# Contiguous rows between the gate and the output projection, and half of the x1*x3 products on GpSimd

## The chip, the cores and the metric

The kernel runs on one core of a Trainium2 chip. The core has five engines that run at the same time, each with a queue that it works off in order: PE (TensorE, the matrix engine; PEld is its weight load, which overlaps with matmuls), DVE (VectorE), ACT (ScalarE), POOL (GpSimd) and SP (which issues the DMAs here). PE writes to PSUM, which has 8 banks of 512 fp32 elements in each of 128 partitions; DVE and ACT read PSUM, and GpSimd works on SBUF alone here. The metric is the device time of one launch in microseconds.

## The reference, cut to what matters

Two layers follow each other, for 4 batches of 6272 positions and 256 channels.

```
f = lb + (1 - lb) * sigmoid(f_logit)
h = f[:, t] * h + (1 - f[:, t]) * x[:, t]        # for t = 0 .. 6271; all h kept
x1, x2, x3 = split(h_all @ w_proj, 3)            # 256 channels each
x2_conv = irfft(rfft(x2) * rfft(filter_fft))     # along the 6272 positions
out = (x1 * x2_conv * x3) @ w_out
```

## The kernel before

Each batch b goes through these steps.

`hgrn(b)` makes the recurrence in 13 chunks of 512 positions (the last has 128). For each chunk, f_logit and x are loaded (L275), ACT makes the sigmoid (L278), GpSimd the product with x (L280), PE turns both so that channels lie on partitions (L287), ACT makes f (L299) and DVE runs the scan over time (L304), once for each half of the channels. From the states, PE then makes x1 and x3 (L315). For each half of the channels, `jb`, ACT copies x1 out of PSUM into `x1s` with a scale (L323), which has two buffers, one for each `jb`; DVE multiplies x3, straight from PSUM, with it and writes `z` in fp16 (L326). `z` holds x1*x3 by channel and time, and has one buffer for each parity of b.

`phase_p(b)` projects to x2 with the time axis split as 128 x 49 (time = 49 m + r). `phase_f1`, `mini` and `units` make the convolution as products with small Fourier matrices, in 16 units of 8 channel pairs; the unit's product with the filter's spectrum is L658 on DVE, and its result goes into `Th` (L673, a copy at L246).

`phase_o(b)` does the rest, in 13 groups of up to four values of r: 12 full groups (rn = 4) and one of a single row (rn = 1). In a group, PE makes the last inverse transform for each row i of the group, with 4 matmuls of 64 partitions by 128 columns a row (L693). Before the change, row i's 128 results go to every rn-th PSUM column, beginning at column i: the order in PSUM is (m i), rows innermost. DVE multiplies with `z`, in which the rows of a group lie side by side too (time = 49 m + r), and writes `ys` (fp32 for PE's use), in the order (m i) as well (L700). PE projects with `w_out` (L710): for row i and each half of the channels, y[:, kh, :, i] is the 128x128 weight of one matmul with 256 columns, so the weight is read at steps of rn elements. ACT or DVE then copies the result out with a scale (L248, L253), and SP stores it (L719). `ys` has two buffers and so has the output.

The order of the work is written out by a planner, `Plan`, before the program is built. Every step is given with its cost on the engines that may do it, its readers and writers, and for PE steps the number of PSUM banks it takes. The planner runs a list schedule with these costs: at each step it takes the operation that can begin first (and among those the one with the longest way to the end), and emits it into its engine's queue. A PE step is emitted only if all that its readers need besides it is already emitted. Work of batch b+1 is thus mixed with units(b) and phase_o(b) where the order allows. The costs are written by hand: phase_o's product is counted at 0.08 + 0.27 us for each row of the group (1.16 us for four), its transform at 0.235 us a row, its projection at 0.34 us a row.

Of the kernel before, what the change touches and what calls it, by code (L numbers as in the profile page):

```python
# [9 lines left out]
F32 = mybir.dt.float32  # L10
# [3 lines left out]
AOP = mybir.AluOpType  # L14
# [12 lines left out]
CH = 512  # L27
# [19 lines left out]
def m0_of(r):  # L47
    return (128 * q_of(r) - r) // Q
# [135 lines left out]
def kernel(  # L184
# [10 lines left out]
    nc = tc.nc  # L195
# [4 lines left out]
    op = plan.op  # L200

    konst = ctx.enter_context(tc.tile_pool(name="konst", bufs=1))
# [22 lines left out]
    FL = konst.tile([128, NX, 4, D], F32, name="FL")  # L225
    fTs = konst.tile([128, 2, CH], F32, name="fTs")
    x1s = konst.tile([128, 2, CH], F32, name="x1s")
    dram = ctx.enter_context(tc.tile_pool(name="dram", bufs=1, space=bass.MemoryType.DRAM))

    H = [dram.tile([TB, 2, 2, UE * 64], F16, name=f"H{u}") for u in range(NU)]  # L230
    psp = ctx.enter_context(tc.tile_pool(name="psp", bufs=1, space=PSUM))
    PS = psp.tile([128, 8, 512], F32, name="PS")
# [25 lines left out]
    def either(n, runs=1.0):  # L258

        return {"ACT": 0.06 + runs * n / 1200.0, "DVE": 0.08 + runs * n / 960.0}  # L260
# [4 lines left out]
    def hgrn(b):  # L265
        z = zt[b % 2]
        for c in range(NCHK):
            t0 = c * CH
            nb = min(CH, S - t0) // 128
            n = nb * 128  # L270
            k = count["x"] % NX
            count["x"] += 1
            xt, ft = XT[:, k, 0:nb], FL[:, k, 0:nb]
            for dst, src, t in ((ft, f_logit, ("ft", k)), (xt, x, ("xt", k))):
                op({"SP": 0.5}, lambda e, dst=dst, src=src, t0=t0, n=n: nc.sync.dma_start(  # L275
                    dst, src[b, t0:t0 + n, :].rearrange("(j p) d -> p j d", p=128)),
                   w=[t], kb=n)
            op({"ACT": 0.1 + 0.213 * nb}, lambda e, ft=ft: nc.scalar.activation(  # L278
                ft, ft, AF.Sigmoid, scale=-1.0), w=[("ft", k)], table="sigmoid")
            op({"POOL": 0.1 + 0.535 * nb}, lambda e, xt=xt, ft=ft: nc.gpsimd.tensor_tensor(  # L280
                xt, xt, ft, op=AOP.mult), r=[("ft", k)], w=[("xt", k)])
            for kh in range(2):
                cols = slice(kh * 128, kh * 128 + 128)

                def turn(e, p, src, cols=cols, nb=nb):
                    for j in range(nb):
                        nc.tensor.transpose(PS[:, p, j * 128:(j + 1) * 128], src[:, j, cols],  # L287
                                            iden[:])
                sT = op({"PE": 0.108 * nb}, lambda e, p, f=turn, s=ft: f(e, p, s),
                        r=[("ft", k), "iden"], w=["qT"], take=1)  # L290
                uT = op({"PE": 0.108 * nb}, lambda e, p, f=turn, s=xt: f(e, p, s),
                        r=[("xt", k), "iden"], w=["qT"], take=1)
                j = count["f"] % 2
                count["f"] += 1
                fT = fTs[:, j, 0:n]
                t1 = HB[kh] + t0
                h = HA[:, t1:t1 + n]
                op({"ACT": 0.13 + n / 1200.0}, lambda e, p, fT=fT, n=n, kh=kh:
                   nc.scalar.activation(fT, PS[:, p, 0:n], AF.Identity,  # L299
                                        scale=nomc[:, kh:kh + 1], bias=1.0),  # L300
                   r=["om"], w=[("fT", j)], src=sT)
                init = 0.0 if c == 0 else HA[:, t1 - 1:t1]
                op({"DVE": 0.07 + 2.25 * n / 1000.0}, lambda e, p, h=h, fT=fT, n=n, init=init:
                   nc.vector.tensor_tensor_scan(h, fT, PS[:, p, 0:n], init, op0=AOP.mult,  # L304
                                                op1=AOP.add),
                   r=[("fT", j)] + ([("hn", kh, c - 1)] if c else []), w=[("hn", kh, c)],
                   src=uT)
            for jb in range(2):
                x13 = []
                for i in range(2):  # L310
                    js = slice(i * 256 + jb * 128, i * 256 + jb * 128 + 128)

                    def mm(e, p, i=i, js=js, t0=t0, n=n):
                        for kh in range(2):
                            nc.tensor.matmul(PS[:, p, 0:n], W13[:, kh, js],  # L315
                                             HA[:, HB[kh] + t0:HB[kh] + t0 + n],
                                             start=(kh == 0), stop=(kh == 1))
                    x13.append(op({"PE": 2 * n / 2400.0}, mm,
                                  r=[("hn", 0, c), ("hn", 1, c), "W13"], w=["qX"], take=1))
                j = count["s"] % 2  # L320
                count["s"] += 1
                xs, zz = x1s[:, j, 0:n], z[:, jb, t0:t0 + n]
                op({"ACT": 0.06 + n / 1200.0}, lambda e, p, xs=xs, n=n: nc.scalar.activation(  # L323
                    xs, PS[:, p, 0:n], AF.Copy, scale=ZS), w=[("x1s", j)], src=x13[0])
                op({"DVE": 0.07 + n / 960.0}, lambda e, p, zz=zz, xs=xs, n=n:
                   nc.vector.tensor_tensor(zz, PS[:, p, 0:n], xs, op=AOP.mult),  # L326
                   r=[("x1s", j)], w=[("z", b % 2, jb, c)], src=x13[1])

    def wraps():
        for kh, cuts in enumerate(((0, 1024, 2560, 4096, E0), (128, 2048, 3584, 5120, S))):  # L330
# [348 lines left out]
    def phase_o(b):  # L679
        zr = zt[b % 2][:].rearrange("p k (m r) -> p k m r", r=Q)  # L680
        tf = Th[:].rearrange("p c a g -> p (c a g)")
        for g, r0 in enumerate(range(0, Q, 4)):
            rn = min(4, Q - r0)

            def inv(e, cb, r0=r0, rn=rn):
                for i in range(rn):
                    r = r0 + i
                    sh = (128 - m0_of(r)) % 128
                    for rr in range(2):
                        c0 = (rr * Q + r) * 128  # L690
                        for p in range(2):
                            ps = slice(64 * p, 64 * p + 64)
                            nc.tensor.matmul(PS[:, cb + p, i:i + rn * 127 + 1:rn],  # L693
                                             tf[ps, c0:c0 + 128], ID[ps, rr, sh:sh + 128],
                                             start=(rr == 0), stop=(rr == 1))
            i1 = op({"PE": 0.235 * rn}, inv, r=[("Th", u) for u in range(NU)] + ["Th"], take=2)
            yk = g % 2
            y = ys[:, yk, :, 0:rn * 128].rearrange("p a (m i) -> p a m i", i=rn)
            op({"DVE": 0.08 + rn * 0.27}, lambda e, cb, y=y, r0=r0, rn=rn:
               nc.vector.tensor_tensor(  # L700
                   y, PS[:, cb:cb + 2, 0:rn * 128].rearrange("p a (m i) -> p a m i", i=rn),
                   zr[:, :, :, r0:r0 + rn], op=AOP.mult),
               r=[("z", b % 2, jb, c) for jb in range(2) for c in range(NCHK)],
               w=[("y", yk)], src=i1)

            def proj(e, ob, y=y, rn=rn):
                po = PS[:, ob:ob + 2].rearrange("m a (r e) -> m (a r) e", e=256)
                for i in range(rn):
                    for kh in range(2):
                        nc.tensor.matmul(po[:, i, :], y[:, kh, :, i], Wo[:, kh, :],  # L710
                                         start=(kh == 0), stop=(kh == 1))
            po = op({"PE": 0.34 * rn}, proj, r=[("y", yk)], take=2)
            k = count["o"] % 2
            count["o"] += 1
            op(either(256 * rn), lambda e, ob, k=k, rn=rn: copy(
                e, osb[k][:, 0:rn, :],
                PS[:, ob:ob + 2].rearrange("m a (r e) -> m (a r) e", e=256)[:, 0:rn, :], OS),
               r=[("x2o", i) for i in range(14)] if k else [], w=[("osb", k)], src=po)
            op({"SP": 0.5}, lambda e, k=k, r0=r0, rn=rn: nc.sync.dma_start(  # L719
                out[b].rearrange("(a r) d -> a r d", r=Q)[:, r0:r0 + rn, :],  # L720
                osb[k][:, 0:rn, :]),
               r=[("osb", k)] + ([("x2o", i) for i in range(14)] if k else []), kb=128 * rn)
# [8 lines left out]
    with tc.manual_schedule():  # L731
        with tc.tile_pool(name="tmp", bufs=1) as tmp:
            prepare(tmp)
            hgrn(0)
            wraps()
            plan.emit()
# [8 lines left out]
        ys = cv.tile([128, 2, 2, 512], F32R, name="ys")  # L745
# [47 lines left out]
```

## Time and profile before

| | us |
|---|---|
| median of 3 runs (lowest 652.3, highest 658.98) | 654.3 |
| the profiled execution | 655.55 |
| span of that execution's trace | 653.4 |
| PE busy in the span | 559.9 (86%) |
| DVE busy | 512.2 (78%) |
| ACT busy | 381.2 (58%) |
| POOL busy | 149.8 (23%) |

The span is what the trace covers; the execution's own time is 2.15 us longer. Busy times are sums over the whole span. An engine's work is the same in kind in each batch but lies in stages with different company: up to about 146 us the filter's transform and the first batch's recurrence and forward transform, then the units of a batch, its phase_o together with the next batch's recurrence, the forward transform, the next units, and so on, and from about 611 us the last phase_o by itself.

### The profile page before, as it was taken

The numbers are of one execution on the slowest core, as the hardware profiler recorded it, in microseconds if no ns is written. First come the engines' busy times: TensorE is split into PE (matmuls) and PEld (weight loads), VectorE is DVE, ScalarE is ACT, GpSimd is POOL, SyncE is SP. The second block draws the span as 40 slices with busy tenths as digits, with TensorE's granted clock in tenths as the row PEclk, the third lists the DMA queues.
The fourth block names the chain that finished last, engine by engine and source line by source line (L and its number), as shares of the span: only waits on it lengthen the run. The fifth ranks groups of instructions, "written<-read, shape, count | busy, mean of one in ns | idle before, by whom it ended". The sixth has DMA issues, their size and how long they took to land.

```text
span 653.4 us, 12392 instructions
## 1 busy us (share of the span) xinstructions
PE 559.9 (86%) x4821; PEld 430.0 (66%) x4821; DVE 512.2 (78%) x576; ACT 381.2 (58%) x490; POOL 149.8 (23%) x161
## 2 busy tenths in 40 slices
PE   3677888977799999897769999988789999968997
PEld 3455555764478886774538986954568887644786
DVE  7768787589978769699889467899987668999632
ACT  3788786794343558793445456964456567833333
POOL 5424420122104223213222132031023220011000
PEclk9989999899979999998898999999899999997898
DMA  8957755556659786435698588134598862055144
GB/s 310 382 178 256 237 164 172 178 170 192 179 167 333 245 300 211 146 129 180 196 266 266 180 276 282 65 97 148 159 258 293 301 219 108 1 162 160 41 186 170
DMA packets 77643, 130.09 MB, mean 199 GB/s; under 512 B 4878, under 2 KB 56146, under 8 KB 77586
## 3 DMA queue, kind: packets, MB, share of 16 engines
q1 hardware_dynamic: 77586, 129.31, 59.9%
q8 instruction: 38, 0.62, 0.4%
q14 instruction: 19, 0.16, 0.1%
HBM read 84.54 MB, written 32.11 MB: 179 GB/s over the span
## 4 chain that ended last, share of the span: by engine, by line
PE 53%; DVE 14%; DMA 13%; ACT 7%; issue 5%; POOL 2%; SPq 1%; DVEq 0%; ACTq 0%; POOLq 0%
PE PS L710 13%; PE PS L287 10%; PE PS L315 8%; DVE PP L658 8%; PE PS L693 6%; DMA FL<-in_f_logit_dram 6%; PE PS L589 5%; PE PS L668 3%; PE PS L604 2%; PE PS L648 2%; DVE HA L304 2%; ACT X L246 2%; DMA XT<-in_x_dram 2%; DMA H<-HA 2%; DMA Hu<-H 2%
## 5 line engine op out<-in xcount | busy, mean ns | idle before, releaser
L280 POOL TENSOR_TENSOR XT<-XT,FL 128x1024 f32<-128x1024 f32 (+1 forms) x52 | 116.4, 2238 | 266.4 <-DMA XT<-in_x_dram 117.6
L658 DVE TENSOR_TENSOR PP<-PS,Hu 98x1008 f16<-98x1008 f32 x128 | 145.6, 1200 | 8.9 <-PE PS L648 3.0
L246 ACT CAST X<-PS 128x784 f16<-128x784 f32 (+2 forms) x92 | 91.7, 1007 | 84.4 <-PE PS L668 77.2
L304 DVE TENSOR_TENSOR_SCAN HA<-fTs,HA,PS 128x512 f16<-128x512 f32 (+1 forms) x96 | 114.6, 1205 | 29.2 <-PE PS L287 20.7
L315 PE MATMUL PS<-HA,W 128*128 128x512 f16 (+1 forms) x416 | 106.5, 376 | 6.0 <-DVE HA L304 3.9
L299 ACT ACTIVATE fTs<-PS,nomc 128x512 f32<-128x512 f32 (+1 forms) x104 | 69.5, 669 | 65.2 <-PE PS L287 46.1
L710 PE MATMUL PS<-Wo,ys 128*128 128x256 f32 x392 | 102.5, 405 | 0.5 <-DVE ys L700 0.5
L710 PEld LDWEIGHTS PS<-Wo,ys 128*128 128x128 f32 x392 | 94.1, 325 | 5.6 <-issue 3.7
L700 DVE TENSOR_TENSOR ys<-PS,z 128x1024 fp32r<-128x1024 f32 (+1 forms) x52 | 60.6, 1178 | 42.0 <-PE PS L693 37.6
L668 PEld LDWEIGHTS <-PP 98*128 98x128 f16 x1024 | 55.8, 105 | 51.4 <-POOL PP L651 20.9
L668 PE MATMUL PS<-VA,PP 98*128 98x98 f16 x512 | 62.7, 220 | 21.7 <-DVE PP L658 9.9
L323 ACT ACTIVATE x1s<-PS 128x512 f32<-128x512 f32 (+1 forms) x104 | 59.0, 576 | 33.1 <-PE PS L315 23.7
L326 DVE TENSOR_TENSOR z<-PS,x1s 128x512 f16<-128x512 f32 (+1 forms) x104 | 66.4, 651 | 14.9 <-ACT x1s L323 10.4
L287 PE MATMUL PS<-iden,FL 128*128 128x128 f32 x392 | 67.1, 296 | 12.4 <-ACT FL L278 12.4
L287 PE MATMUL PS<-iden,XT 128*128 128x128 f32 x392 | 65.3, 289 | 8.9 <-POOL XT L280 7.3
L278 ACT ACTIVATE FL<-FL 128x1024 f32<-128x1024 f32 (+1 forms) x52 | 52.5, 1010 | 22.2 <-DMA FL<-in_f_logit_dram 22.1
L287 PEld LDWEIGHTS PS<-iden,XT 128*128 128x128 f32 x392 | 48.1, 148 | 25.2 <-POOL XT L280 10.4
L315 PEld LDWEIGHTS <-W 128*128 128x128 f16 x416 | 37.4, 100 | 39.3 <-issue 15.3
L668 PE MATMUL PS<-VB,PP 98*128 98x98 f16 x512 | 62.5, 220 | 0.0
L287 PEld LDWEIGHTS PS<-iden,FL 128*128 128x128 f32 x392 | 49.3, 152 | 19.6 <-ACT FL L278 9.8
L648 PE MATMUL PS<-HA,FT 64*128 64x512 f16 x256 | 41.8, 402 | 20.8 <-ACT X L246 19.2
L693 PE MATMUL PS<-ID,X 64*128 64x128 f16 x784 | 51.3, 309 | 1.0 <-ACT X L248 0.5
(90 smaller groups left out, 583.4 us busy)
## 6 DMA issues: line engine op xcount, KB each, us to landing
Hu<-H SPq DMA_DIRECT2D x64, 392.0 KB
FL<-in_f_logit_dram SPq DMA_DIRECT2D x48, 512.0 KB
XT<-in_x_dram SPq DMA_DIRECT2D x48, 512.0 KB
out_dram<-X SPq DMA_DIRECT2D x24, 512.0 KB
out_dram<-osb SPq DMA_DIRECT2D x24, 512.0 KB
HA<-in_moe_filter_fft_dram SPq DMA_DIRECT2D x12, 512.0 KB
HA<-HA SPq DMA_DIRECT2D x16, 384.0 KB
H<-HA SPq DMA_DIRECT2D x16, 196.0 KB
```

The lines of the kernel that those rows point to most:

```text
L246: nc.scalar.copy(dst, src)
L280: op({"POOL": 0.1 + 0.535 * nb}, lambda e, xt=xt, ft=ft: nc.gpsimd.tensor_tensor(xt, xt, ft, op=AOP.mult), r=[("ft", k)], w=[("xt", k)])
L287: nc.tensor.transpose(PS[:, p, j * 128:(j + 1) * 128], src[:, j, cols], iden[:])
L299: nc.scalar.activation(fT, PS[:, p, 0:n], AF.Identity, scale=nomc[:, kh:kh + 1], bias=1.0),
L304: nc.vector.tensor_tensor_scan(h, fT, PS[:, p, 0:n], init, op0=AOP.mult, op1=AOP.add),
L315: nc.tensor.matmul(PS[:, p, 0:n], W13[:, kh, js], HA[:, HB[kh] + t0:HB[kh] + t0 + n], start=(kh == 0), stop=(kh == 1))
L326: nc.vector.tensor_tensor(zz, PS[:, p, 0:n], xs, op=AOP.mult),
L658: nc.vector.tensor_tensor(PP[:TB, k, o, :, :, 1:64], px.unsqueeze(1).broadcast_to([TB, 2, UE, 63]), hh[:, :, :, 1:64], op=AOP.mult)
L668: nc.tensor.matmul(PS[:, ib + o, pr * TB:(pr + 1) * TB], PP[:TB, k, o, n, 2 * pr:2 * pr + 2, :], v[:TB], start=(n == 0), stop=(n == 1))
L693: nc.tensor.matmul(PS[:, cb + p, i:i + rn * 127 + 1:rn], tf[ps, c0:c0 + 128], ID[ps, rr, sh:sh + 128], start=(rr == 0), stop=(rr == 1))
L700: nc.vector.tensor_tensor(y, PS[:, cb:cb + 2, 0:rn * 128].rearrange("p a (m i) -> p a m i", i=rn), zr[:, :, :, r0:r0 + rn], op=AOP.mult),
L710: nc.tensor.matmul(po[:, i, :], y[:, kh, :, i], Wo[:, kh, :], start=(kh == 0), stop=(kh == 1))
```

## The change

Two things are changed. In `phase_o`, the rows of a group no longer lie interleaved: row i's results go to 128 adjoining PSUM columns, and `ys` has the order (i m), so that the weight of one projection matmul is contiguous. The product on DVE runs over the same elements in the same order, m outside and i inside, through views of the new layout. In `hgrn`, the product x1*x3 of the first half of the channels (jb = 0) is no longer made by DVE from PSUM: ACT copies x3 out of PSUM into a new tile `x3s` (one buffer), and GpSimd multiplies `x3s` with `x1s` and writes `z`. The second half stays on DVE. The planner is given costs for the two new steps, and its other costs are not changed.

```diff
@@ -225,6 +225,7 @@
     x1s = konst.tile([128, 2, CH], F32, name="x1s")
+    x3s = konst.tile([128, CH], F32, name="x3s")
@@ -322,9 +323,17 @@
                 xs, zz = x1s[:, j, 0:n], z[:, jb, t0:t0 + n]
                 op({"ACT": 0.06 + n / 1200.0}, lambda e, p, xs=xs, n=n: nc.scalar.activation(
                     xs, PS[:, p, 0:n], AF.Copy, scale=ZS), w=[("x1s", j)], src=x13[0])
-                op({"DVE": 0.07 + n / 960.0}, lambda e, p, zz=zz, xs=xs, n=n:
-                   nc.vector.tensor_tensor(zz, PS[:, p, 0:n], xs, op=AOP.mult),
-                   r=[("x1s", j)], w=[("z", b % 2, jb, c)], src=x13[1])
+                if jb:
+                    op({"DVE": 0.07 + n / 960.0}, lambda e, p, zz=zz, xs=xs, n=n:
+                       nc.vector.tensor_tensor(zz, PS[:, p, 0:n], xs, op=AOP.mult),
+                       r=[("x1s", j)], w=[("z", b % 2, jb, c)], src=x13[1])
+                else:
+                    x3 = x3s[:, 0:n]
+                    op({"ACT": 0.06 + n / 1200.0}, lambda e, p, x3=x3, n=n:
+                       nc.scalar.copy(x3, PS[:, p, 0:n]), w=["x3s"], src=x13[1])
+                    op({"POOL": 0.1 + 2.15 * n / 1000}, lambda e, zz=zz, xs=xs, x3=x3:
+                       nc.gpsimd.tensor_tensor(zz, x3, xs, op=AOP.mult),
+                       r=[("x1s", j), "x3s"], w=[("z", b % 2, jb, c)])
@@ -690,15 +699,15 @@
-                            nc.tensor.matmul(PS[:, cb + p, i:i + rn * 127 + 1:rn],
+                            nc.tensor.matmul(PS[:, cb + p, i * 128:(i + 1) * 128],
                                              tf[ps, c0:c0 + 128], ID[ps, rr, sh:sh + 128],
                                              start=(rr == 0), stop=(rr == 1))
             i1 = op({"PE": 0.235 * rn}, inv, r=[("Th", u) for u in range(NU)] + ["Th"], take=2)
             yk = g % 2
-            y = ys[:, yk, :, 0:rn * 128].rearrange("p a (m i) -> p a m i", i=rn)
+            y = ys[:, yk, :, 0:rn * 128].rearrange("p a (i m) -> p a m i", i=rn)
             op({"DVE": 0.08 + rn * 0.27}, lambda e, cb, y=y, r0=r0, rn=rn:
                nc.vector.tensor_tensor(
-                   y, PS[:, cb:cb + 2, 0:rn * 128].rearrange("p a (m i) -> p a m i", i=rn),
+                   y, PS[:, cb:cb + 2, 0:rn * 128].rearrange("p a (i m) -> p a m i", i=rn),
                    zr[:, :, :, r0:r0 + rn], op=AOP.mult),
```

## Rows read from the trace of the kernel before

**Rows 1.** Page, part 1: busy us, share of the span, instructions of each engine.

```profile
PE 559.9 (86%) x4821; PEld 430.0 (66%) x4821; DVE 512.2 (78%) x576; ACT 381.2 (58%) x490; POOL 149.8 (23%) x161
```

**Rows 2.** Busy time by stage: stretch and length, engines, clock granted, DMA share, GB/s.

```profile
core 0: us, PE busy (x) PEld busy (x) DVE busy (x) ACT busy (x) POOL busy (x), PEclk, DMA share, GB/s
185.00:262.00 77.00, 76.13 (x562) 61.61 (x560) 60.44 (x62) 43.75 (x64) 22.34 (x12) 0.98 0.76 256
...
345.00:407.70 62.70, 61.70 (x467) 51.28 (x465) 42.20 (x44) 34.11 (x48) 16.73 (x8) 0.97 0.75 254
437.00:471.70 34.70, 26.63 (x295) 16.06 (x296) 34.70 (x38) 14.81 (x22) 4.74 (x15) 0.96 0.47 151
471.70:547.20 75.50, 73.27 (x585) 59.75 (x584) 55.84 (x59) 44.70 (x63) 20.33 (x12) 1.00 0.77 256
```

**Rows 3.** Timeline of the last phase_o: start and length in us, count, idle before.

```profile
634.69 1.94 PEld L710 LDWEIGHTS PS<-Wo,ys 128*128 128x128 f32 x8 [0.21 <-issue]
634.70 2.15 PE L710 MATMUL PS<-Wo,ys 128*128 128x256 f32 x8
634.81 1.22 DVE L700 TENSOR_TENSOR ys<-PS,z 128x1024 fp32r<-128x1024 f32 x1 [1.83 <-PE PS L693]
...
636.77 0.77 PEld L693 LDWEIGHTS <-X 64*128 64x128 f16 x16
636.77 1.05 PE L693 MATMUL PS<-ID,X 64*128 64x128 f16 x16
...
637.75 2.14 PE L710 MATMUL PS<-Wo,ys 128*128 128x256 f32 x8
```

**Rows 4.** Timeline of DVE in the first mixed stage: two products in a row.

```profile
217.11 2.53 DVE L700 TENSOR_TENSOR ys<-PS,z 128x1024 fp32r<-128x1024 f32 x2
```

**Rows 5.** L710's loads at 640.8 and 647.8 us (min/median/max ns), the one-row L693's loads.

```profile
L710 PEld LDWEIGHTS PS<-Wo,ys x8: 309/329/332, 640.8 to 642.4; 128*128 128x128 f32 x8
...
L710 PEld LDWEIGHTS PS<-Wo,ys x3: 189/208/334, 647.8 to 648.2; 128*128 128x128 f32 x3
...
645.93 0.11 PEld L693 LDWEIGHTS <-X 64*128 64x128 f16 x4
```

**Rows 6.** Timeline of L519, matmuls of L710's shape with contiguous weights, and their loads.

```profile
26.85 1.19 PE L519 MATMUL PS<-afs,rot 128*128 128x256 f32 x8
...
26.83 1.01 PEld L519 LDWEIGHTS PS<-afs,rot 128*128 128x128 f32 x8
```

**Rows 7.** By tile, ns min/median/max; then groups by form, busy us and mean ns.

```profile
L326 DVE TENSOR_TENSOR z<-PS,x1s x104: 280/682/697, 20.7 to 611.3; 128x512 f16<-128x512 f32 x96, 128x128 f16<-128x128 f32 x8
L700 DVE TENSOR_TENSOR ys<-PS,z x52: 679/1224/1227, 188.0 to 646.3; 128x1024 fp32r<-128x1024 f32 x48, 128x256 fp32r<-128x256 f32 x4
...
L251 DVE CAST f<-PS x15: 407/691/726, 18.2 to 48.4; 128x512 fp32r<-128x512 f32 x14, 128x128 fp32r<-128x128 f32 x1
...
L323 ACT ACTIVATE x1s<-PS x104: 277/597/948, 20.1 to 611.0; 128x512 f32<-128x512 f32 x96, 128x128 f32<-128x128 f32 x8
...
L246 ACT CAST X<-PS 128x784 f16<-128x784 f32 x64 | 51.7, 810 | 77.3 <-PE PS L668 77.2
L280 POOL TENSOR_TENSOR XT<-XT,FL 128x1024 f32<-128x1024 f32 x48 | 113.4, 2363 | 258.0 <-DMA XT<-in_x_dram 117.6 <-ACT FL L278 76.2 <-PE PS L287 27.8
L280 POOL TENSOR_TENSOR XT<-XT,FL 128x256 f32<-128x256 f32 x4 | 2.9, 727 | 8.4 <-PE PS L693 4.4 <-ACT FL L278 4.0
```

**Rows 8.** Busy time by stage of L326 alone, on DVE.

```profile
185.00:262.00 77.00, 12.53 (x19) 0.98 0.76 256
...
345.00:407.70 62.70, 8.62 (x13) 0.97 0.75 254
437.00:471.70 34.70, 5.87 (x10) 0.96 0.47 151
471.70:547.20 75.50, 11.60 (x18) 1.00 0.77 256
```

**Rows 9.** Waits, 185 to 262 us: who waited for whom, us in total, times, longest.

```profile
POOL XT L280 <- DMA XT<-in_x_dram: 22.7, 3, 16.4
```

## Prediction

> **What bounds the kernel now.** I read the busy shares first [rows 1], and in them only that PE is the fullest engine and DVE the second. Such a share is a mean over unlike stages, so the second view is the busy time by stage [rows 2]. It shows two kinds of stage, repeated for each batch. While the gate and the output projection run (phase_o), mixed with the next batch's recurrence, PE is busy 76.1 of 77, 61.7 of 62.7 and 73.3 of 75.5 us, and DVE 60.4, 42.2 and 55.8: PE sets the end. In the spectral units DVE does (34.7 of 34.7 us in the row shown). The last phase_o has no recurrence beside it, and its timeline shows the bare beat [rows 3]: a projection (L710) starts at 634.70 and the next at 637.75, 3.05 us apart. PE fills this with 2.15 us of L710 and some 1 us of transforms (L693), while the product on DVE takes 1.22 us after 1.83 us of idling. A batch has 12 full groups of four rows and one group of one row.
>
> **The two PE edits.** The group of one row is a trial of the change that the kernel already carries: with rn = 1, stepping by rn is contiguous, so its weights and PSUM columns lie as the change lays all of them. In a full group an L710 weight load takes 329 ns in the median; in the window with the one-row group the shortest takes 189 [rows 5]. Eight full L710 loads fill 1.94 us, 240 ns each. What the matmuls then take is shown by another line of the same shape (128x128 fp32 weights, 256 columns) with contiguous weights: eight in 1.19 us, loads in 1.01 us, 126 ns each [rows 6]. I take 130 ns for a load and its matmul, against the 240: 8 x 0.11 = 0.88 us less in a group. For L693, sixteen strided ones load in 0.77 us, 48 ns each, and take 1.05 us; the four contiguous ones load in 0.11 us, 28 ns each [rows 3, 5]. With the matmuls paced by their loads, 16 x 0.020 = 0.32 us less. Together 1.2 us of PE in each full group, 14 us in a batch; one-row groups stay as they are.
>
> **What this costs DVE.** L700 still walks m outside and i inside, because z lies so. Its PSUM reads and its writes to ys now jump 512 bytes at each element, where both were contiguous. No row shows such a product, so I bound it. From below: 1.22 us, unchanged. Jumping reads alone seem free: the fp32 copies into f read PSUM at 1 KB steps and write runs of four, and 512 elements take 691 ns, like the 682 ns of the contiguous product L326 [rows 7]. From above: the ACT copies into Th (X in the row) change their SBUF line every four elements, at 256-byte steps, and 784 elements still take 810 ns. L326's two sizes, 682 ns for 512 and 280 for 128, give 1.05 ns an element and about 0.15 us fixed; with that fixed cost a line change hides in (810 - 150) / 196 = 3.4 ns, which would make 1024 x 3.4 ns + 0.15 = 3.6 us. Nearest is one instruction, the copy into f with a single row: 128 fp32 elements, each written to a place of its own and read with jumps, take 407 ns, about (407 - 155) / 128 = 1.97 ns each. The one-row L700 points there too: 256 elements with jumping reads of z take 679 ns or more, 2.1 ns each. I take 1024 x 1.97 + 155 = 2.17 us, 0.95 more than now, and keep 1.22 and 3.6 for the range.
>
> [...]
>
> **Half of the products.** Of 26 L326 in a batch, 13 leave DVE: 12 x 0.682 + 0.280 = 8.5 us. ACT gets as many copies at L323's price (0.597 us [rows 7]), 7.5 us in a batch. It is busy 43.8 of 77 us in the first mixed stage [rows 2], so I cost them at nothing; without that cover all 7.5 would show. GpSimd gets 13 products. L280's two sizes, 2.363 and 0.727 us [rows 7], give 2.13 ns an element and 0.18 us fixed, so 1.27 us for 512 and 16 us in a batch, beside 22.3 us busy of 77. The wait that this adds: x3s is one buffer, so the ACT copy of a chunk waits for the GpSimd product of the chunk before, with ACT's sigmoids and PSUM copies queued behind it; on GpSimd the next L280 is behind the product, and PE's transposes wait for that. Nothing reads z before the batch's phase_o, so the product's own lateness is free except there. No DMA is moved, and SP's queue stays.
>
> **The sum, against the profiled execution's 653.4 us span.** Last phase_o: DVE now sets the beat. Two L700 in a row take 2.53 us [rows 4], 40 ns more each than one alone, so 2.21 us in place of 3.05, with PE at about 1.5 to 1.8 beside it: 12 x 0.84 = 10 us less.
>
> The three mixed stages: DVE loses half of its L326 there (12.5, 8.6 and 11.6 us [rows 8]) and gains 12 x 0.95 = 11.4, so it comes to 65.5, 49.3 and 61.4 us, above PE's 62, 47.5 and 59. If DVE is filled to 92%, the stages take 71, 53.5 and 66.5: 24 us less. If instead PE waits in each group for the whole 0.95 us, because the written order still counts the product at 1.16 us, 1.2 - 0.95 = 0.25 us in each of 36 groups are left: 9 us less. I take the middle, 17.
>
> Units: where the row shows DVE full, the products inside shrink by half of 5.9 us [rows 8], 3 us less. First recurrence and filter transform: 0, with 4 us either way as a guess, because its order is drawn anew.
>
> 10 + 17 + 3 = 30 less makes a span of 623.4. The profiled execution took 655.55, 2.15 more than its span, and stands 1.25 over the median of 654.3; so 624 us, and by its own bounds (9 to 24, and 4 either way) about 612 to 637. Its chance is 0.55.
>
> **Rivals.**
> *L700 pays nothing.* Then PE still sets the beat, at 1.8 us with its latencies: 15 less in the last phase_o, and 12 of the 14 us in each of the others, where the DMA share of 0.76 would come near 0.9. With the units, 54 less: 600 us. For it: free jumping reads and free runs of four. Against it: both single-element rows. Chance 0.15.
> *GpSimd and ACT jam.* An L280 at the head of GpSimd waits for its XT load, three times and 22.7 us in all in the first mixed stage [rows 9]. If a product stands behind it, x3s stays full, and the next ACT copy holds up ACT's queue, with the PSUM banks that PE needs. At one such wait of 6 us not hidden in each of three stages: 642 us. For it: one x3s. Against it: the order is drawn up with GpSimd's price in it. Chance 0.15.
> *L700's writes cost up to the upper bound: slower.* At 3.6 us the last phase_o beats at 3.64 (+7) and DVE needs 83, 66 and 79 us in the mixed stages, +13 when full and +24 at 95%; less the units, 671 to 682, about 676 us. It turns from gain to loss where L700 reaches some 2.9 us. For it: steps of 512 bytes, which no row has. Against it: 1.97 ns in the nearest one. Chance 0.10.
> *Weight loads don't speed up*, if the 189 ns came from the end of PE's queue and not from the stride. PE then stays the bound, and only the units' 3 us are left: 651 us. Against it: the contiguous loads 126 ns apart [rows 6]. Chance 0.05.
>
> A lower clock is no case of its own: where DVE sets the end today and PE has work for 26.6 of 34.7 us, 0.96 of the clock was granted [rows 2], and PE's new slack under DVE is about what such a loss takes.
>
> **The numbers.** 598 to 648 us holds most of the first three cases (0.55, two thirds of 0.15 and nearly all of the jam's 0.15) and leaves out the slow ones. Within 1% (about what a measurement of this kernel can tell from no change) lie the dead weight loads, the bad end of the jam and the mild end of the slow case, 0.10; slower by over 1%, the rest of the slow case, 0.08; faster 0.82.
>
> **What would show it.** Right: L710 loads near 190 ns and eight matmuls in about 1.2 us; sixteen L693 in some 0.7 us; L700 near 2.2 us; the last phase_o beating at 2.2 us with DVE without gaps; DVE ahead of PE in the mixed stages. Wrong: L700 at 1.2 or above 2.9 us, L710 still 240 ns each, ACT waiting for GpSimd at the x3s copies, or a PE clock well under 0.9 in the mixed stages.

## The result and the profile after

The changed kernel takes 631.8 us in the median (629.5 to 642.6), against 655.6 us for the kernel before in the same comparison: a ratio of 0.9625, 95% interval 0.9553 to 0.9697. The 642.6 us is one execution in a slower state, which the ratio leaves out. The prediction was 624 us, 598 to 648, faster with 0.82. The profiled execution took 632.6 us with a span of 630.9.

The page's first part, busy time and share by engine, answers to [rows 1]:

```profile
PE 510.1 (81%) x4821; PEld 372.7 (59%) x4821; DVE 520.8 (83%) x529; ACT 392.2 (62%) x532; POOL 214.0 (34%) x214
```

PE has lost 50 us of busy time and DVE has gained 9: 33 us of products left it, its gate products grew by 35 (95.3 us in place of 60.6), and the rest are copies that the planner gave to it. DVE is now the fullest engine. Lines are shifted: L700 is now L709, L710 is L719, L693 is L702, L326 is L328, and the GpSimd product is L335. The groups of instructions by form (count, busy us, mean ns of one, idle time before and what ended it) give the new prices; they answer to [rows 5, 7]:

```profile
L709 DVE TENSOR_TENSOR ys<-PS,z 128x1024 fp32r<-128x1024 f32 x48 | 92.8, 1977 | 5.5 <-PE PS L702 3.1 <-ACT X L249 0.8 <-POOL z L335 0.6
...
L335 POOL TENSOR_TENSOR z<-x3s,x1s 128x512 f16<-128x512 f32 x48 | 61.4, 1279 | 119.6 <-ACT x3s L333 116.3 <-PE PS L677 3.2
...
L719 PEld LDWEIGHTS PS<-Wo,ys 128*128 128x128 f32 x392 | 50.9, 193 | 29.6 <-DVE ys L709 15.8 <-issue 6.6 <-ACT FL L279 2.6
```

The timeline of the last phase_o (start, length, count) answers to [rows 3]:

```profile
603.47 20.37 DVE L709 TENSOR_TENSOR ys<-PS,z 128x1024 fp32r<-128x1024 f32 x11 [1.18 <-PE PS L702]
...
605.62 1.19 PE L719 MATMUL PS<-Wo,ys 128*128 128x256 f32 x8
...
606.73 0.45 PEld L702 LDWEIGHTS <-X 64*128 64x128 f16 x16
606.74 0.62 PE L702 MATMUL PS<-ID,X 64*128 64x128 f16 x16
```

The view merges instructions of one line under the form of the first: these eleven are ten products of four rows and the one-row product, which takes 0.70 us. So the products start (20.37 - 0.70) / 10 = 1.97 us apart in the mean, as long as one takes, and PE waits for them, 2.1 us in these 20.37: DVE sets the beat, as forecast. To see where the whole 22.5 us of span went, I cut the trace at two marks in each batch: the first spectrum product (L667) and the first gate product. "Units" runs from the one to the other, "mixed" from there to the next batch's first spectrum product (for the last batch, to the end).

| us | start | units 1 to 4 | mixed 1 to 3, last phase_o | span |
|---|---|---|---|---|
| before | 146.6 | 41.4, 59.3, 49.5, 43.4 | 105.5, 80.4, 85.9, 41.4 | 653.4 |
| changed | 146.7 | 60.8, 55.7, 55.2, 47.0 | 79.8, 80.1, 73.2, 32.4 | 630.9 |
| layout alone | 145.1 | 41.7, 60.0, 49.4, 42.4 | 103.2, 72.9, 82.5, 31.3 | 628.5 |

In the changed kernel the mixed stages and the last phase_o lose 48 us together, and the units, which should have gained, take 25 us more. The busy times by stage of the changed kernel (columns as in [rows 2]), units 1 and mixed 1 to 3, and the scans alone (L305) in units 1 to 3:

```profile
146.70:207.50 60.80, 44.76 (x441) 30.68 (x441) 51.82 (x49) 28.19 (x39) 21.27 (x24) 0.84 0.70 212
207.50:287.30 79.80, 69.14 (x684) 55.36 (x681) 65.39 (x54) 54.90 (x70) 25.08 (x16) 0.95 0.61 209
...
343.00:423.10 80.10, 70.38 (x701) 55.58 (x695) 68.35 (x57) 57.60 (x75) 28.95 (x19) 1.00 0.65 222
...
478.30:551.50 73.20, 64.13 (x667) 52.03 (x666) 64.31 (x53) 51.32 (x64) 21.72 (x14) 1.00 0.60 211
```

```profile
146.70:207.50 60.80, 14.01 (x11) 0.84 0.70 212
287.30:343.00 55.70, 10.06 (x8) 0.97 0.68 201
423.10:478.30 55.20, 7.50 (x6) 0.85 0.60 179
```

The next batch's recurrence has moved. Units 1 to 3 now hold 25 scans, 31.6 us; before, the same count of L304 was 17, 21.2 us, and lay otherwise:

```profile
146.60:188.00 41.40, 2.32 (x2) 0.93 0.60 182
293.50:352.80 59.30, 13.84 (x11) 0.86 0.72 214
433.20:482.70 49.50, 5.05 (x4) 0.97 0.51 154
```

The layout kernel has 2, 11 and 4, as before. A units stage is longest where it holds the most scans (11: 59.3 and 60.8 us). The scans are only part of the 25 us: over the four units stages DVE is busy 192.1 us in place of 180.7, and idle 26.6 in place of 12.9. The spectrum products account for much of the idling, with 13.3 us of waiting for PE where they had 3.0 (before, then changed):

```profile
L658 DVE TENSOR_TENSOR PP<-PS,Hu 98x1008 f16<-98x1008 f32 x128 | 145.6, 1200 | 8.9 <-PE PS L648 3.0 <-issue 2.4 <-ACT X L246 1.9
```

```profile
L667 DVE TENSOR_TENSOR PP<-PS,Hu 98x1008 f16<-98x1008 f32 x128 | 146.5, 1200 | 20.5 <-PE PS L657 13.3 <-DMA Hu<-H 5.4 <-ACT x3s L333 0.8
```

In the mixed stages neither PE (87%, 88%, 88%) nor DVE (82%, 85%, 88%) is full.

### The profile page after: what moved, and what is told of

Read it like the earlier page. It is cut to its first block, busy times and chain, and to the rows that moved or that the text cites. A ratio compares the mean times of both kernels' runs of the same rounds, so it can differ in the third digit from the quotient of the medians.

```text
span 630.9 us, 12466 instructions
## 1 busy us (share of the span) xinstructions
PE 510.1 (81%) x4821; PEld 372.7 (59%) x4821; DVE 520.8 (83%) x529; ACT 392.2 (62%) x532; POOL 214.0 (34%) x214
## 5 line engine op out<-in xcount | busy, mean ns | idle before, releaser
L667 DVE TENSOR_TENSOR PP<-PS,Hu 98x1008 f16<-98x1008 f32 x128 | 146.5, 1200 | 20.5 <-PE PS L657 13.3
L305 DVE TENSOR_TENSOR_SCAN HA<-fTs,HA,PS 128x512 f16<-128x512 f32 (+1 forms) x96 | 114.3, 1201 | 16.0 <-PE PS L288 7.6
L316 PE MATMUL PS<-HA,W 128*128 128x512 f16 (+1 forms) x416 | 108.8, 377 | 9.2 <-DVE HA L305 4.0
L335 POOL TENSOR_TENSOR z<-x3s,x1s 128x512 f16<-128x512 f32 (+1 forms) x52 | 63.2, 1216 | 122.8 <-ACT x3s L333 119.5
L709 DVE TENSOR_TENSOR ys<-PS,z 128x1024 fp32r<-128x1024 f32 (+1 forms) x52 | 95.3, 1879 | 6.3 <-PE PS L702 3.9
L677 PE MATMUL PS<-VA,PP 98*128 98x98 f16 x512 | 62.7, 223 | 25.2 <-DVE PP L667 10.8
L719 PE MATMUL PS<-Wo,ys 128*128 128x256 f32 x392 | 60.8, 298 | 19.4 <-DVE ys L709 17.7
L719 PEld LDWEIGHTS PS<-Wo,ys 128*128 128x128 f32 x392 | 50.9, 193 | 29.6 <-DVE ys L709 15.8
L288 PEld LDWEIGHTS PS<-iden,XT 128*128 128x128 f32 x392 | 46.8, 147 | 29.1 <-POOL XT L281 13.9
L657 PE MATMUL PS<-HA,FT 64*128 64x512 f16 x256 | 44.4, 425 | 18.6 <-ACT X L247 17.7
L598 PE MATMUL PS<-W,HA 128*128 128x256 f16 x392 | 47.1, 282 | 7.4 <-DMA HA<-HA 6.8
```

The lines of the kernel that those rows point to most:

```text
L316: nc.tensor.matmul(PS[:, p, 0:n], W13[:, kh, js], HA[:, HB[kh] + t0:HB[kh] + t0 + n], start=(kh == 0), stop=(kh == 1))
L335: nc.gpsimd.tensor_tensor(zz, x3, xs, op=AOP.mult),
L667: nc.vector.tensor_tensor(PP[:TB, k, o, :, :, 1:64], px.unsqueeze(1).broadcast_to([TB, 2, UE, 63]), hh[:, :, :, 1:64], op=AOP.mult)
L677: nc.tensor.matmul(PS[:, ib + o, pr * TB:(pr + 1) * TB], PP[:TB, k, o, n, 2 * pr:2 * pr + 2, :], v[:TB], start=(n == 0), stop=(n == 1))
L709: nc.vector.tensor_tensor(y, PS[:, cb:cb + 2, 0:rn * 128].rearrange("p a (i m) -> p a m i", i=rn), zr[:, :, :, r0:r0 + rn], op=AOP.mult),
```

## The experiments

Several kernels can be compared at one order of the work. The planner's prices for phase_o were not changed with the layout, so the kernel before and "layout alone" have the same order (A below), and the changed kernel, "products alone", "ys alone" and "PSUM alone" have another one (B). In the traces the instructions of every engine come in the same sequence within each of these two sets. Trials that give the planner another price, buffer or dependence have an order of their own.

**The two halves of the change.**

```diff
 # e1_rows_only: the three lines of phase_o as changed; hgrn as before
 # e2_products_only: hgrn as changed; the three lines of phase_o as before
```

> Only the layout of phase_o is changed; all products x1*x3 stay on DVE. Theory (the gain comes from PE's shorter phase_o, and DVE then sets the end there): the last phase_o beats at 1.85 to 2.05 us as in the changed kernel, about 9 us less; in the mixed stages DVE carries 12 x 0.76 us more without relief, 69, 51 and 65 us of work, so some 6 us less in all; about 640 us. Rival (the relief of DVE by GpSimd makes the gain of the mixed stages): the last phase_o alone gains, about 646 us.

> Only the products x1*x3 of the first half move to ACT and GpSimd; phase_o keeps its old layout. Theory: PE stays the bound of phase_o, and the time falls only where DVE was full, in the units: about 3 us less, 650 to 653 us. Rival (the relief lets scans move into the units and shortens the mixed stages): 10 us less or more, 645 us. Jam rival (one x3s holds up ACT's queue): no gain or slower, 655 to 662 us.

Layout alone: 630.5 us, ratio 0.9628 (0.9581 to 0.9676). Products alone: 663.0 us, ratio 1.0136 (1.0079 to 1.0192), slower. So the layout gives the whole gain. My theory missed the first by 10 us and the second by as much: the layout is worth more, and the products less, than I thought. The jam rival (655 to 662) comes nearest to the second, but ACT waited only 4.5 us for GpSimd's products there, so a jam is not shown in it. In the layout kernel the last phase_o is 10.1 us shorter and the mixed stages 2.3, 7.5 and 3.4 (table), with DVE busy 88%, 90% and 88% of them:

```profile
186.80:290.00 103.20, 92.08 (x832) 71.35 (x833) 90.98 (x84) 69.97 (x94) 29.44 (x15) 0.96 0.68 226
...
350.00:422.90 72.90, 64.20 (x656) 51.49 (x656) 65.26 (x57) 52.73 (x65) 17.65 (x10) 1.00 0.67 230
...
472.30:554.80 82.50, 73.28 (x713) 57.60 (x712) 72.28 (x66) 57.60 (x72) 17.60 (x10) 0.98 0.59 207
```

**Which jump costs the gate product.**

```diff
 # e5_ys_only: as changed, but
-    nc.tensor.matmul(PS[:, cb + p, i * 128:(i + 1) * 128],
+    nc.tensor.matmul(PS[:, cb + p, i:i + rn * 127 + 1:rn],
-    y, PS[:, cb:cb + 2, 0:rn * 128].rearrange("p a (i m) -> p a m i", i=rn),
+    y, PS[:, cb:cb + 2, 0:rn * 128].rearrange("p a (m i) -> p a m i", i=rn),
 # e6_psum_only: as changed, but
-    y = ys[:, yk, :, 0:rn * 128].rearrange("p a (i m) -> p a m i", i=rn)
+    y = ys[:, yk, :, 0:rn * 128].rearrange("p a (m i) -> p a m i", i=rn)
```

> As changed, but the transforms still write PSUM columns at steps of rn: only ys is row by row. Product on DVE: reads contiguous, writes at 512-byte steps. Theory (single-element writes cost it): the product stays at 1.98 us; L719-type projections stay at 1.2 us for eight, the transforms go back to 1.05 us for sixteen. The last phase_o then beats at 1.2 + 0.81 = about 2.0 us or a little over, and PE has 12 x 0.36 = 4 us more in each batch beside a DVE that is as full as in the changed kernel: 632 to 640 us. Rival (the jumping PSUM reads cost it): product 1.22 us, and the time 620 to 630 us.

> As changed, but ys keeps the interleaved order, so the projection's weights are read at steps of rn; only the PSUM columns are row by row. Product on DVE: reads at 512-byte steps, writes contiguous. Theory (reads are free): the product takes 1.22 us, the transforms 0.6 us for sixteen, the projections 2.15 us for eight; the last phase_o beats at about 2.6 to 2.7 us, PE remains the bound of the mixed stages with 4 us less in each: about 635 to 643 us. Rival (reads cost it): the product takes 1.9 us or more.

645.2 us (0.9859, 0.9813 to 0.9904) and 648.3 us (0.9919, 0.9886 to 0.9952). The groups by form, first with jumping writes and contiguous reads, then with jumping reads and contiguous writes:

```profile
L709 DVE TENSOR_TENSOR ys<-PS,z 128x1024 fp32r<-128x1024 f32 x48 | 93.9, 1982 | 10.2 <-PE PS L702 6.4 <-ACT X L249 1.9 <-ACT osb L249 0.7
```

```profile
L719 PEld LDWEIGHTS PS<-Wo,ys 128*128 128x128 f32 x392 | 94.7, 325 | 7.5 <-issue 2.2 <-DVE ys L709 1.6 <-DVE HA L305 0.9
...
L709 DVE TENSOR_TENSOR ys<-PS,z 128x1024 fp32r<-128x1024 f32 x48 | 57.7, 1215 | 32.2 <-PE PS L702 23.7 <-issue 4.2 <-ACT X L249 2.9
```

The writes to `ys` cost all of it, 1982 ns; the jumping PSUM reads nothing, 1215 ns. Both times are 5 us above my upper ends; I had reckoned from the changed kernel's 631.8 and took each edit's worth as small. At order B the edits are worth 18 us (ys: 663.0 to 645.2) and 15 us (PSUM columns: 663.0 to 648.3), and 31 together; at order A both together are worth 23.

**Is it the single buffer, or where the recurrence lies?**

```diff
 # e3_two_x3s
-    x3s = konst.tile([128, CH], F32, name="x3s")
+    x3s = konst.tile([128, 2, CH], F32, name="x3s")      # used in turn, c % 2
 # e8_held_back: the loads of f_logit and x in hgrn
-    w=[t], kb=n)
+    r=[("Th", 12)] if b and c < 2 else [], w=[t], kb=n)
```

> As changed, with two buffers for x3s in turn. So far: the layout alone gave 630.5 us, the products alone 663.0, both together 631.8; so the products on GpSimd cost about what they take off DVE. Theory S (the order: with DVE relieved, the planner moves the next recurrence into the units, where ACT waits for its loads in front of the units' copies): a second x3s changes little, 627 to 636 us. Theory J (one x3s jams ACT and GpSimd): 618 to 625 us.

> As changed, but from the second batch on the loads of the first two chunks of the next recurrence wait for the 13th unit, so that the units run nearly alone. Theory S: the first units take 41 to 45 us from first product to first gate in place of 61, the mixed stages get longer by less than that, and the time falls to 618 to 627 us. Theory J: the jam moves along with the recurrence, into a fuller mixed stage: 632 us or more.

Two x3s: 629.6 us, 0.9632 (0.9598 to 0.9665), not told apart from the changed kernel's 0.9625; theory J's 618 to 625 fails in the planned order, in which ACT waits 2.8 us in all for GpSimd's products. The waits stand at the x1s copies, and x1s for jb = 0 still had one buffer. Held back: 646.8 us, 0.9884 (0.9837 to 0.9931), slower than the changed kernel. Its units take 42 to 44 us each, as theory S said, but the mixed stages 97.7, 100.3 and 98.8. So, in these two orders, the recurrence inside the units is not the harm that I took it for, and that part of theory S falls. Theory J's 632 us or more holds in number; its sign, ACT waiting for GpSimd's products, grew only from 2.8 to 6.8 us, too little for 15. The order was redrawn too, and the next trials show such a step for prices alone, so what the holding back itself costs stays open.

**What the written order is worth.**

```diff
 # e4_priced_plan (as changed) and e7_rows_priced (layout alone), planner prices only
-    op({"PE": 0.235 * rn}, inv, ...
+    op({"PE": 0.14 * rn}, inv, ...
-    op({"DVE": 0.08 + rn * 0.27}, ...
+    op({"DVE": 0.11 + rn * 0.46}, ...
-    op({"PE": 0.34 * rn}, proj, ...
+    op({"PE": 0.29 * rn}, proj, ...
 # e12_before_repriced (kernel before): 0.2, 0.15 + rn * 0.27 and 0.48 in these places
```

> As changed, but the planner counts phase_o as the chip runs it: product 0.11 + 0.46 us a row (1.95 for four; was 1.16), transform 0.14 us a row (was 0.235), projection 0.29 us a row (was 0.34). The prediction let PE wait in part because the order still counted the product at 1.16 us. If that wait is real, 5 to 10 us less than the changed kernel: 622 to 627 us; if the order hardly matters there, 628 to 635 us.

> The layout change alone (all products on DVE, 630.5 us so far), with the same corrected prices for the planner. If the written order makes PE wait for the product: 620 to 626 us. If DVE's work is what sets the mixed stages there (69, 51 and 65 us of it): no change, 627 to 634 us.

> The kernel before, with nothing changed but three prices of the planner (phase_o's product 0.15 + 0.27 us a row, transform 0.2, projection 0.48), near what its trace shows. It does the same work in another order. It measures what redrawing the order is worth by itself: if the order is a small thing, 648 to 660 us; if it is worth as much as the corrected prices made it in the layout kernel (16 us), outside of that.

627.1 us (0.9572, 0.9521 to 0.9624), 646.2 us (0.9882, 0.9820 to 0.9944) and 660.6 us (1.0089, 1.0063 to 1.0114). New prices made one order a little better, if anything (the intervals overlap), one 16 us worse and one 6 us worse. The first two sets are truer in all three prices; in the third the transform's price of 0.80 us for four rows is further than the old 0.94 from the 1.05 it takes. The work was the same each time but for five to seven copies that went from DVE to ACT. So an order redrawn cost this kernel 6 and 16 us, clear of noise, as much as the steps that I summed, and truer prices don't assure a gain. The slower orders were granted a lower mean clock too (0.922 for e7, 0.943 for the layout alone), but e4, the fastest of the three, had 0.924, so the clock does not rank them.

**The engine of the products at a given order.** One kernel keeps order B and makes all products on DVE: where B has the GpSimd product, DVE multiplies straight from PSUM, and the ACT copy is left out. The bank may by then hold a later matmul's values, so its output is not the reference's; the work has the same kinds and counts. The other keeps order A and issues the copy and the GpSimd product where A has the DVE product.

```diff
 # e10_after_order_dve
-    nc.scalar.copy(x3, PS[:, p, 0:n]), w=["x3s"], src=x13[1])
+    at.append(p), w=["x3s"], src=x13[1])
-    nc.gpsimd.tensor_tensor(zz, x3, xs, op=AOP.mult),
+    nc.vector.tensor_tensor(zz, PS[:, at[0], 0:n], xs, op=AOP.mult),
 # e11_rows_order_pool, jb = 0
-    nc.vector.tensor_tensor(zz, PS[:, p, 0:n], xs, op=AOP.mult)
+    nc.scalar.copy(x3s[:, 0:n], PS[:, p, 0:n])
+    nc.gpsimd.tensor_tensor(zz, x3s[:, 0:n], xs, op=AOP.mult)
```

> The order of the changed kernel (its planner input is the same), but where it has the ACT copy of x3 nothing is issued, and where it has the GpSimd product DVE multiplies straight from PSUM, as before. So only the engine of half of the products differs. So far: both together 631.8 us, the layout alone (in an order of its own) 630.5, held-back loads 646.8, corrected prices 627.1 with and 646.2 without the GpSimd products. Theory O (GpSimd does take work off the path, and the redrawn order gives it back): in this order DVE pays 52 x 0.65 = 34 us more in stages where it is 82 to 90% busy, so the time is 640 us or more. Theory N (the products' place costs nothing either way): 628 to 636 us.

> The other way round: the order of the kernel with the layout change alone, but at each product of the first half ACT copies x3 and GpSimd multiplies. Theory O: DVE loses 34 us of work and nothing else moves, so the time falls from 630.5 to 615 to 625 us. Theory N: 627 to 635 us. If the unplanned copies on ACT and products on GpSimd, with one x3s, get into the way (theory J): 636 us or more.

| new layout | products on DVE | half on ACT and GpSimd |
|---|---|---|
| order A | 630.5 | 659.4 (1.0084, 1.0051 to 1.0117) |
| order B | 643.3 (0.9823, 0.9787 to 0.9859) | 631.8 |

In B the kernel with GpSimd is 11.5 us faster, about what theory O said. But the trial has a wait of its own: its DVE product reads a bank that the plan has already given on, and PE's next matmuls into that bank wait for it. PE waits 10.8 us in all for these products, most of it in the row below, and 0.4 us for all x1*x3 products in the layout kernel:

```profile
PE PS L315 <- DVE z L334: 7.7, 8, 2.2
```

How much of the 11.5 us is GpSimd's help, and how much the trial's own wait, is not shown. In A GpSimd adds 29 us: unplanned, the chain through one x1s for jb = 0 gets into the way. Waits over the whole span of e11 (who waited for whom, us in all, times, longest):

```profile
DVE z L328 <- ACT x1s L324: 31.8, 19, 3.3
...
DVE HA L305 <- PE PS L288: 23.5, 17, 3.7
...
ACT x1s L324 <- POOL z L331: 20.8, 16, 2.4
```

ACT's x1 copy stands for GpSimd's product of the chunk before, with DVE's other products behind it; the scans wait 23.5 us for their transposes, 10.8 in the layout kernel. So a jam such as the one that I gave 0.15 exists at this order, though at the x1s copies; the x3s copies, which I had named, wait for no GpSimd product. In the planned order ACT's wait for GpSimd is 2.8 us. That order with all products on DVE is 12.8 us slower than A (643.3 against 630.5), the trial's own wait included. What is shown is that each order does best with the products that it was planned for, and that the two planned kernels are level.

**The stores.** The changed kernel's ACT waits for output stores: 13.6 us in all over the span, 8 of them in the last phase_o.

```diff
 # e14_three_out_priced: e4_priced_plan and a third output buffer
-            k = count["o"] % 2
+            k = count["o"] % 3
...
+               cv.tile([128, 4, 256], F32, name="osb2")]
```

> The changed kernel with the corrected planner prices (627.1 us) and a third output buffer. In the changed kernel ACT waits 13 us in all for output stores, and the chain that ends last runs through stores 497.9 to 505.0, 521.1 to 525.9 and through the whole last phase_o from 611 us. If the two buffers bind there: 617 to 624 us, and the last phase_o's products follow each other without ACT's waits. If only DVE does: 624 to 630 us.

615.2 us, 0.9388 (0.9365 to 0.9412): the fastest kernel here, 1.9% under the same prices with two buffers by the ratios. Its profiled execution took 624.3 us, so its stages are not compared; but in it the last phase_o has no wait for a store left and still takes 32.1 us, 32.4 in the changed kernel. ACT's output copies there, and their only wait:

```profile
L249 ACT ACTIVATE osb<-PS x8: 1024/1026/1028, 594.5 to 617.5; 128x1024 f32<-128x1024 f32 x8
...
  PE PS L719: 17.1, 12
```

So the stores did not bind the last phase_o; DVE did. Whether the gain is the mixed stages' waits for stores or once more a luckier order stays open.

## Why the prediction was right, point by point

**PE's two edits** were right in kind, and a little small in size: 0.96 + 0.43 = 1.39 us less in a full group, where I took 1.2. L719's loads take 193 ns (forecast: near 190) and eight matmuls 1.19 us (1.2); sixteen L702 take 0.62 us (some 0.7) with loads of 0.45 us, 28 ns each. The one-row group was a true trial of the change.

**The gate product** was right in kind and 9% off in size: 1.98 us where I took 2.17, so 0.76 more than before where I took 0.95, and 1.97 us from one to the next in a row where I took 2.21. The writes are what costs it, by e5 and e6: 1982 ns with jumping writes and contiguous reads, 1215 ns the other way round. The upper bound of 3.6 us was an estimate from 196 runs of four in 810 ns on ACT [rows 7]; that each of these runs is a change of line, as that estimate has it, was not shown. In PSUM the two engines differ: sixteen transforms took 1.05 us into columns at steps of four and 0.62 us into adjoining ones, while DVE's jumping PSUM reads cost nothing by e6 (1215 ns, 1218 before).

**The last phase_o** came out near the sum, 9.0 us less (forecast 10), because two errors met. The beat is shorter than forecast, but ten groups follow it and not twelve: from the third product to the one-row product it takes 19.7 us in place of 29.8. The start and the end lose 1.0 us: the first product starts at 598.55 and the third only at 603.47 (4.9 us, 4.5 before), and from the start of the one-row product it takes 7.7 us to the end (7.1 before). PE had idled 2.1 us before the first projection, and from 602 to 604 us the granted clock was 0.50; sixteen L702 took 1.04 us from 602.39, and 0.62 from 604.89.

**The mixed stages** were 17 less by the prediction, 9 to 24, with DVE's relief in it. In the changed kernel they are 38.7 less, outside of these ends, and the units give 25.1 back. The layout alone gives 13.2 there, without the relief; for that case I had expected some 6 (e1). So that the 13.2 lies near 17 is in part luck: the layout was worth more and the relief less than I summed. DVE fills the stages to 88 to 90% with the layout alone and to 82 to 88% in the changed kernel, not 92%. The clock granted there was 0.95 to 1.00, so the sign "well under 0.9" did not come.

**The products** are the step that failed. I let them shorten the units by 3 us, counted the relief of DVE into the mixed stages, and wrote "0, with 4 us either way" for a redrawn order, in the first stage alone. The units became 25 us longer, because the new steps and their prices redrew the order: more of the scans lie in them, and DVE idles 13.6 us longer. The mixed stages became shorter by about as much beyond the layout's share. The products' sum is nothing: 631.8 against 630.5; how it divides between GpSimd's help and the order stays open. Mixed stages and units together gained 13.6 us and not 20. These 6.4 us and the 1.0 of the last phase_o make nearly all of the 7.5 us by which the span missed 623.4. The time stayed within the sum's own bounds, 612 to 637. The direction was earned, since the layout alone gives the gain (e1); that the number came so close was helped by errors that offset each other.

## What to carry to other kernels

Look in the trace for an instance in which the changed stride or shape already occurs, like the one-row group here: its rows gave L719's loads to a few per cent (189 ns against 193) and the saving of both PE edits to within a sixth. Where an order is drawn by a list schedule, any new operation or price redraws all of it, and that alone cost this kernel up to 16 us; compare a step at a fixed order before crediting it, look in that trace for waits that the borrowed order itself brings (10.8 us here), and give a redrawn order its own term and range in the sum. Off-loading half of the products from DVE, with PE nearly as full, bought a different order here and no time.

## What the runs showed of the hardware

The cost of a jumping write was about 0.75 ns an element ((1982 - 1215) / 1024 from e5 and e6), less than the 0.93 that the 128-element copy had suggested. In a row, such products started 1.97 us apart in the mean, about what one takes.

Jumping reads were free from PSUM (1215 ns in e6, 1218 in the kernel before) and seem not to be from SBUF: the one-row product reads single fp16 elements of `z` 98 bytes apart, with PSUM and `ys` contiguous, and takes 679 ns or more for 256 elements [rows 7]. By L326's two sizes (0.15 us fixed, 1.05 ns an element) it would take 0.42 us, an estimate. Not every run of four was free either: DVE's copies into `X` write runs of four fp16 and take 1470 ns for 1024 elements, 1215 for the contiguous ones into `HA` (kernel before); their PSUM reads jump too, at the 1 KB steps that cost the copies into `f` nothing (691 ns for 512 elements, 682 for L326 [rows 7]).
